# Chunks 0 and 1 of a banded-attention kernel computed as dense blocks on TensorE, with the gate weights decoded first

## The chip, the core and the metric

The kernel runs on one core of a Trainium2 chip. The metric is device time in microseconds of one execution of the whole program. A core has five engines that run their own instruction queues in order and wait for each other by semaphores: TensorE (PE; its weight loads are listed as PEld), VectorE (DVE), ScalarE (ACT), GpSimd (POOL) and SyncE (SP, which here only issues DMAs). Matmul results go to PSUM, which this kernel divides into three pools, `ps_a` (3 buffers), `ps_h` (3) and `ps_o` (2).

## What is computed

Inputs are q, k, v of shape (8 batches, 8 heads, 576 positions, 64) and the weights of a gated feed-forward network, all float32 at the reference; the kernel's weights arrive as float64 bit patterns and are decoded on chip.

```
def _attn_ref(q, k, v):
    q_d, k_d, v_d = means of q, k, v over groups of 4 positions       # 144 positions
    out_up = repeat(softmax(q_d k_d^T / 8) v_d, 4)                    # "coarse" part
    mask = |i - j| < 4
    out_local = softmax(where(mask, q k^T / 8, -1e9)) v               # "banded" part
    return out_up + out_local

x = attn rows, one row of 8 heads * 64 = 512 numbers per token, 4608 tokens
xn = x / sqrt(mean(x*x) + 1e-6) * rms_g
out = (silu(xn @ w_gate) * (xn @ w_val)) @ w_out                       # 512 -> 1536 -> 512
```

## The kernel before

The 4608 tokens are cut into 18 chunks of 256. A chunk is not 256 neighbours: a "unit" takes positions 4u to 4u+3 of each of 16 segments of 36 positions, for two batches, and chunk c holds units 2c and 2c+1 (`j` = 0, 1). Each chunk has three parts.

**Coarse part** (`Coarse`, one object per batch and head pair, 32 in all, 8 of them for batches 0 and 1, which chunks 0 to 4 need): `scores` (PE, L499), `peak` and `scale` (DVE, L508, L513), `powers` (ACT, L518), `turn` (PE transposes, L527), `copy` (ACT, L534), `values` (PE, L541), `invert`, `scaled` (DVE) and `store` (a DMA from ACT's queue to a DRAM tile `up`). Its inputs are sums of q and k, and of v, over 4 positions. For batches 0 and 1 `OpeningSums` loads the four addends (`raw_qk`, 1.18 MB each, `raw_v`) into places that the decoded weights take later (`wo`, `wv`, `wg`), adds q and k by identity products on PE (`add`, L408) with a copy on ACT (L420), and v on POOL and DVE (L429). For later batches POOL's accumulating DMAs add them.

**Banded part** (`Attention`): per chunk 8 products of 128x896 on DVE (`score`, L757) with a sum each (`score_sum`, L761), a softmax on small tiles, then the weighted values as 7 terms per output, made by ACT (`value_scalar`, L804), DVE and POOL (`value`, L811), and added by DVE (`value_sum`, L830), for chunks 0 and 1 by identity products on PE (L826). `load_up` (ACT's queue, L839) reads the coarse results back from DRAM, `add_up` (DVE, L845) adds them, then come `squares` (ACT, L855), `mean` (PE, L862), `rms` and three Newton steps `root` (DVE or POOL), `norm` (DVE, L894), `turn` (PE, L906), `high` (ACT, L910) and `low` (DVE, L914), which leave the transposed chunk as a rounded part `xh` and its rest `xl`.

**Feed-forward part** (`Forward`): for each of 12 blocks f of 128 hidden columns: `first(f, 0)` (the gate product, 12 matmuls of 256 columns, L975), `tanh` (ACT, L982), `first(f, 1)` (the value product, 12 matmuls), `gate` and `product` (DVE, L985, L990), `high` (ACT, L996), `low` (DVE or POOL, L999), and `second(f)` two blocks later (6 matmuls of 512 columns, L1010). At the end two copies on ACT (L1017) and two stores of the output (L1020).

**Weights.** 36 pieces of 0.52 MB (24 of `w_gate` and `w_val`, 12 of `w_out`) are loaded by SP and decoded (`load_weight`): `scale` on ACT (L254), `last_bits` on POOL (L264), `join` on DVE (L271), `high` on ACT (L283, L281), `split` on DVE or POOL (L295, L293, L291). Block f = 0 of chunk 0 needs the 8 pieces of its group; every third piece of the first 24 is one of `w_out`. A rounded weight may be written once the users of its place (`used`) are done.

**Order.** A planner (`Plan`) decides the order of chunks 0 to 2: each piece of work is a task with an engine, a cost, a due time and its inputs and buffers; the planner walks through time and starts the earliest possible task, the one with the smallest due time among equals. The engines then run the queues that result. `due` holds the chunks' due times, `MB` the planner's time for a megabyte of DMA. From chunk 3 on the order is written out by hand and arranged by the compiler's own scheduler.

## Time and profile before

| | us |
|---|---|
| median of 3 runs (1148.75, 1149.18, 1151.49) | 1149.18 |
| the profiled execution | 1145.97 |
| its span, from first to last instruction | 1144.2 |
| first gate matmul of chunk 0 starts at | 108.89 |
| store of chunk 0's output issued at | 188.17 |
| store of chunk 1's, 2's, 3's, 4's output issued at | 256.08, 318.72, 375.88, 446.80 |

In the profile a line such as `L975 PE MATMUL ps_h<-xh,wg 128*128 128x256 f32 x1728 | 348.2, 283 | ...` is a group of instructions: source line, engine, operation, tile written and tiles read, shape, count, then busy time in us and the mean duration of one in ns, then how long the engine was idle just before them and who ended that. A stage table gives for each stretch of time the busy time of every engine, the TensorE clock that was granted (1.00 is full) and the share of the DMA engines in use. The chain of waits is followed back from the last instruction. Durations of instructions on one engine overlap a little, so that the groups of a stretch add up to more than its busy time.

### The profile page before, as it was taken

What the parts mean: (1) busy time and instruction counts of PE and PEld (TensorE: products, weight loads), DVE (VectorE), ACT (ScalarE), POOL (GpSimd) and SP (SyncE); (2) the same over time, 40 slices, a digit from 0 to 9 for tenths busy, and PEclk for the clock granted to TensorE, in tenths of its full rate; (3) what the DMA queues carried; (4) which work ended last, traced back from release to release, by engine and by line L of the source; (5) the groups of instructions that cost most, each with busy time, mean ns of one, the idle gap of its engine ahead of it and who ended that gap; (6) DMA issues with size and microseconds to landing.
All of it is one profiled execution on the core that took longest, in us unless ns stands there. A gap on an engine that the chain in (4) does not pass through costs nothing.

```text
span 1144.2 us, 22238 instructions
## 1 busy us (share of the span) xinstructions
PE 1082.0 (95%) x8002; PEld 990.2 (87%) x8002; DVE 927.7 (81%) x1869; ACT 624.1 (55%) x2284; POOL 255.7 (22%) x317
## 2 busy tenths in 40 slices
PE   6883799999999899999999999999999999999998
PEld 4772698888899899999999999999999999999997
DVE  6787898778889989797979797979798989887432
ACT  1574673747392847474747474747475573837221
POOL 1554562334221211111111111101011020201000
PEclk9885999999999999999999999999999999999999
DMA  9985482446535353535263535222231313220000
GB/s 264 301 275 170 102 227 76 95 101 149 127 87 117 99 115 88 115 87 115 83 120 87 115 88 114 78 64 75 66 91 46 105 52 99 68 58 20 1 19 19
DMA packets 76815, 119.59 MB, mean 105 GB/s; under 512 B 26784, under 2 KB 36256, under 8 KB 76704
## 3 DMA queue, kind: packets, MB, share of 16 engines
q1 hardware_dynamic: 47520, 97.34, 28.8%
q0 software_dynamic: 8640, 15.93, 9.0%
q10 hardware_dynamic: 20544, 4.89, 2.0%
q8 instruction: 63, 1.03, 0.4%
q14 instruction: 48, 0.39, 0.1%
HBM read 106.33 MB, written 11.80 MB: 103 GB/s over the span
## 4 chain that ended last, share of the span: by engine, by line
PE 76%; DVE 9%; DMA 8%; ACT 3%; issue 3%; SPq 1%; POOL 1%; ACTq 0%; DVEq 0%; POOLq 0%
PE ps_h L975 46%; PE ps_o L1010 23%; PE ps_a L541 2%; DMA wg<-in_v_sum_dram 2%; DMA qk<-in_qk_sum_dram 2%; PE ps_a L499 2%; ACT prod L804 1%; DMA vs<-in_v_sum_dram 1%; PE ps_a L906 1%; DVE prod L757 1%; DVE o_sb L271 1%; PE ps_a L527 1%; DMA kv<-in_k_pad_dram 1%; DVE sc L761 1%; DMA up<-o_g 1%
## 5 line engine op out<-in xcount | busy, mean ns | idle before, releaser
L1010 PE MATMUL ps_o<-wo,hs 128*128 128x512 f32 x1296 | 356.0, 399 | 4.2 <-POOL hs L999 3.7
L975 PE MATMUL ps_h<-xh,wg 128*128 128x256 f32 x1728 | 348.2, 283 | 4.8 <-ACT xh L910 2.3
L975 PE MATMUL ps_h<-xh,wv 128*128 128x256 f32 x1728 | 343.0, 281 | 4.6 <-DVE sil L985 4.5
L975 PEld LDWEIGHTS ps_h<-xh,wg 128*128 128x128 f32 x1728 | 282.9, 190 | 14.2 <-ACT xh L910 3.0
L975 PEld LDWEIGHTS ps_h<-xh,wv 128*128 128x128 f32 x1728 | 281.9, 189 | 10.8 <-DVE sil L985 6.9
L804 ACT ACTIVATE prod<-kv,sc 128x64 f32<-128x64 f32 x1072 | 281.7, 408 | 13.0 <-DVE sc L795 4.8
L1010 PEld LDWEIGHTS ps_o<-wo,hs 128*128 128x128 f32 x1296 | 221.9, 188 | 41.4 <-POOL hs L999 6.2
L975 PE MATMUL ps_h<-xl,wg 128*128 128x256 f32 x864 | 244.8, 283 | 0.1
L975 PE MATMUL ps_h<-xl,wv 128*128 128x256 f32 x864 | 241.5, 280 | 0.0
L982 ACT ACTIVATE sil<-ps_h 128x256 f32<-128x256 f32 x216 | 82.9, 384 | 233.9 <-PE ps_h L975 208.8
L811 POOL TENSOR_TENSOR prod<-sc,kv 128x256 f32<-128x256 f32 x144 | 116.4, 843 | 397.4 <-DVE sc L795 175.4
L985 DVE SCALAR_TENSOR_TENSOR sil<-sil,ps_h 128x256 f32<-128x256 f32 x216 | 89.7, 415 | 103.1 <-ACT sil L982 91.0
L975 PEld LDWEIGHTS ps_h<-xl,wg 128*128 128x128 f32 x864 | 164.1, 190 | 6.9 <-issue 1.3
L975 PEld LDWEIGHTS ps_h<-xl,wv 128*128 128x128 f32 x864 | 163.6, 189 | 1.8
L996 ACT ACTIVATE hs<-sil 128x256 fp32r<-128x256 f32 x216 | 89.5, 416 | 136.9 <-DVE sil L990 122.4
L757 DVE TENSOR_TENSOR prod<-q_t,kv 128x896 f32<-128x896 f32 x140 | 151.7, 1086 | 5.6 <-DMA q_t<-in_q_band_dram 5.2
L830 DVE TENSOR_REDUCE x_t<-prod 128x128 f32<-128x896 f32 x128 | 136.8, 1077 | 23.6 <-ACT prod L804 16.4
L761 DVE TENSOR_REDUCE sc<-prod 128x14 f32<-128x896 f32 x144 | 154.5, 1077 | 0.4
L999 DVE TENSOR_TENSOR hs<-sil,hs 128x256 fp32r<-128x256 f32 x196 | 91.4, 466 | 29.5 <-ACT hs L996 29.2
L990 DVE SCALAR_TENSOR_TENSOR sil<-sil,ps_h 128x256 f32<-128x256 f32 x216 | 89.9, 416 | 8.1 <-PE ps_h L975 6.4
L362 POOL DMA_DIRECT2D qk<-in_qk_sum_dram x36 | 32.2, 895 | 187.3 <-DMA qk<-in_qk_sum_dram 111.8
L811 DVE TENSOR_TENSOR prod<-sc,kv 128x128 f32<-128x128 f32 (+2 forms) x144 | 69.5, 515 | 1.6 <-PE ps_o L826 0.8
(118 smaller groups left out, 984.3 us busy)
## 6 DMA issues: line engine op xcount, KB each, us to landing
kv<-in_k_pad_dram SPq DMA_DIRECT2D x72, 320.0 KB
kv<-in_v_pad_dram SPq DMA_DIRECT2D x72, 320.0 KB
qk<-in_qk_sum_dram POOLq DMA_DIRECT2D x36, 288.0 KB, 5.3
out_dram<-o_sb SPq DMA_DIRECT2D x36, 256.0 KB
q_t<-in_q_band_dram SPq DMA_DIRECT2D x70, 128.0 KB
vs<-in_v_sum_dram POOLq DMA_DIRECT2D x36, 144.0 KB, 3.5
qk<-in_qk_sum_dram SPq DMA_DIRECT2D x12, 288.0 KB
wo<-in_qk_sum_dram SPq DMA_DIRECT2D x2, 1152.0 KB
```

Of the source, the lines that this page charges most:

```text
L757: nc.vector.tensor_tensor(out=pr, in0=bcast(q[:, s0:s0 + 2], 2, NO), in1=window(k, s0), op=ALU.mult)
L761: nc.vector.tensor_reduce(out=self.sc[:, j, par, s0:s0 + 2], in_=self.pr[i], axis=AX.X, op=ALU.add,)
L804: nc.scalar.activation(out=self.pr[i][:, o, s], in_=self.v[j, par][:, s0 + s + o], func=AF.Copy, scale=p[:, s, o:o + 1],)
L811: (nc.vector if engine == "DVE" else nc.gpsimd).tensor_tensor(out=self.pr[i][:, a:b], in0=bcast(p[:, :, a:b].rearrange("p s o -> p o s"), ...
L830: nc.vector.tensor_reduce(out=self.x[j][:, s0:s0 + 2, par], in_=pr.rearrange("p o s d -> p s d o"), axis=AX.X, op=ALU.add,)
L975: nc.tensor.matmul(out=self.p[f][:, t], lhsT=wi(f)[:, 0, k], rhs=xi[:, k], start=(n == 0), stop=(n == 3 * KT - 1),)
L982: nc.scalar.activation(out=self.sil[f], in_=self.p[f][:, 0], func=AF.Tanh, scale=0.5)
L985: nc.vector.scalar_tensor_tensor(out=self.sil[f], in0=self.sil[f], scalar=1.0, in1=self.p[f][:, 0], op0=ALU.add, op1=ALU.mult,)
L990: nc.vector.scalar_tensor_tensor(out=self.sil[f], in0=self.sil[f], scalar=0.5, in1=self.p[f][:, 1], op0=ALU.mult, op1=ALU.mult,)
L996: nc.scalar.activation(out=self.hs[f][:, 0], in_=self.sil[f], func=AF.Copy)
L999: (nc.gpsimd if engine == "POOL" else nc.vector).tensor_tensor(out=self.hs[f][:, 1], in0=self.sil[f], in1=self.hs[f][:, 0], op=ALU.subtract,)
L1010: nc.tensor.matmul(out=self.o[j], lhsT=lhs[:, cols], rhs=rhs(f)[:, 0], start=(f == 0 and i == 0), stop=(f == NF - 1 and i == 2),)
```

## The change

- **Banded part of chunks 0 and 1** (new class `Dense`). For one batch b, a chunk has 128 tokens (16 segments of 8 positions). For each batch and head pair: `gather` (ACT) picks the 128 queries of the chunk out of `raw_qk`; `scores` (PE) makes, for each of the two heads, a 128x256 block of all queries against the 16 keys around each of the 16 segments: a product that writes the mask (0 or -1e30), a small one that masks the left edge of the sequence (chunk 0 only), and the product of q with k, read with strides from `raw_qk`; `peak` (DVE, two reductions and a scale), `powers` (ACT, two exponentials with their sums), `turn_a` (PE, four transposes), `copy` (ACT, 128x512) and `values` (PE, four products with v). v is loaded by 66 small DMAs of up to 16 rows x 8 heads x 64 numbers (`load_v`). The masks and a 0/1 spread matrix are made on POOL.
- **Coarse part for batches 0 and 1.** Results stay on chip (in a free part of `wo`'s place); `spread_up` adds up each chunk's rows by a product with the spread matrix. They are still stored to `up` for chunks 2 to 4, now by SP. The sums of q and k are made by three DVE additions of 128x576 instead of products on PE and copies on ACT.
- **Normalisation of chunks 0 and 1.** A token is one row, so its mean square comes from ACT's sum, without the `mean` product; `turn` multiplies with strided columns of the identity, which also puts the tokens of two batches in the order that later stages expect.
- **Weights.** The order of pieces is four of `w_gate` for f = 0 to 3, four for f = 4 to 7, four of `w_val` for f = 0 to 3, then four of `w_out`, and so on. The gate product of a block waits for gate pieces alone, the value product for value pieces. `scale` now waits, as `high` did, for the users of the weight's place; `used["wv"]` and `used["wo"]` hold all dense scores and value products of both chunks.
- **Planner:** due times 62, 118, 173 instead of 70, 125, 180, `MB` 3.6 instead of 3.1, some costs.

Not in the core below: the planner's numbers, `peak`, `powers`, `invert`, `scaled`, `squares`, `norm`.

```diff
+    class Dense:
+        def plan(self, warm_bufs, warmed):
...
+            for b in range(2):
+                for hp in range(KT):
+                    n = 4 * b + hp
+                    tag = ("ps_a", "ps_h")[n % 2]
+                    ps, pt, A, AT = [buf(tag) for _ in range(2)], buf(tag), buf("dense_a"), buf("dense_t")
+                    gather = task("ACT", 0.25, lambda b=b, hp=hp: self.gather(b, hp), at - 10, [sums_.got])
+                    scores = task(
+                        "PE", 1.15, lambda b=b, hp=hp, tag=tag: self.scores(b, hp, tag), at, [gather, rounded, stores, warmed, *self.order[-1:]],
+                        allocs=[*ps, A, AT], uses=[mask, self.bufs[3], *warm_bufs, sa, sl, *self.more],
+                    )
+                    used["wo"].append(scores)
+                    used["wv"].append(scores)
...
+        def masks(self):
+            nc.gpsimd.memset(m, 0.0)
+            for pattern, base, sign in (... four half-planes ...):
+                nc.gpsimd.affine_select(
+                    out=m, in_=m, pattern=pattern, compare_op=ALU.is_ge, fill=NEVER, base=base, channel_multiplier=sign,
+                )
...
+        def scores(self, b, hp, tag):
+            for par, ps in enumerate(self.s[b, hp]):
+                nc.tensor.matmul(out=ps, lhsT=warm["some"][:, :P], rhs=d.mask_r, start=True, stop=False)
...
+                k = bass.AP(tensor=tensor, offset=at - 1, ap=[part, [UPP, NSEG], [1, 4], [step, FAC]])
+                rows = slice(par * D, (par + 1) * D)
+                nc.tensor.matmul(
+                    out=ps, lhsT=self.q[b, hp][rows], rhs=k[rows],
+                    start=False, stop=True,
+                )
...
+        def spread_up(self, b):
+            up = self.up[b] = ps_a.tile([P, DM], FP32, name="ps_a")
+            for hp in range(KT):
+                og = self.coarse[4 * b + hp].og
+                for c in range(2):
+                    at = D * (1 - c)
+                    nc.tensor.matmul(
+                        out=up[:, hp * P:(hp + 1) * P], lhsT=(self.prev or self).made[self.c][:HALF, at:at + P], rhs=og[:, :, c],
+                        start=(c == 0), stop=(c == 1),
+                    )
...
-            for t in range(2):
-                p = buf(tag)
-                add = task("PE", 2.3, lambda t=t: self.add(t), at, got[:1], allocs=[p])
+            for j in range(1, FAC):
+                add = task(
+                    "DVE", 0.68, lambda j=j: self.add(j), at, [got[0], add],
+                    allocs=[self.qk_buf] if j == 1 else [], uses=[self.qk_buf],
+                )
...
-            nc.scalar.dma_start(
+            (nc.sync if self.b < 2 else nc.scalar).dma_start(
                 out=up_dram[self.b // 2][self.b % 2, self.hp].rearrange("t (c p) d -> p t c d", c=2), in_=self.og,
             )
...
+    order = [(0, i) for i in (*range(4), *range(8, 12), *range(4, 8))] + [(1, f) for f in range(4)]
+    order += [(0, i) for i in range(12, 16)] + [(1, f) for f in range(4, 8)]
+    order += [(0, i) for i in range(16, 24)] + [(1, f) for f in range(8, 12)]
...
-        own = joined[:24] if n >= 24 else used["wo"] if n not in gained else used["wg"] + used["wv"]
+        own = joined[:24] if n >= 24 else used["wo"] if n not in gained else used["wv" if gained[n] % 8 // 4 else "wg"]
...
+        scaled = task("ACT", 0.67, scale, at, [got, *own], allocs=[w], uses=[raw])
```

**How the queues change, at three places.** First SP's queue (DMA issues) around the last loads of the opening's sums (`in_qk_sum`, `in_v_sum`). Before, the value rows of chunk 0's band (`kv`) follow, then the first weight pieces (`in_w_...`):

```order
L396 DMA wv_0_203<-in_qk_sum_dram 128x4x576
L402 DMA wg_0_192<-in_v_sum_dram 72x4x512
L568 DMA kv<-in_v_pad_dram 128x1x640 x4
L250 DMA wg_1_295<-in_w_gate_dram 128x1024
L250 DMA wg_1_295<-in_w_val_dram 128x1024
L250 DMA wg_1_337<-in_w_out_dram 128x1024
```

Now, with the coarse stores (`up<-wo`) on the same queue and the small value loads (16x8x64):

```order
L564 DMA up<-wo_0_115 72x4x64
L408 DMA wg_0_340<-in_v_sum_dram 72x4x512
L402 DMA wv_0_183<-in_qk_sum_dram 128x4x576
L408 DMA wg_0_340<-in_v_sum_dram 72x4x512
L564 DMA up<-wo_0_115 72x4x64
L1078 DMA kv<-in_v_pad_dram 16x8x64 x16
L564 DMA up<-wo_0_115 72x4x64
L1078 DMA wv_0_166<-in_v_pad_dram 16x8x64 x8
L1078 DMA wv_0_183<-in_v_pad_dram 16x8x64 x8
L254 DMA wg_1_548<-in_w_gate_dram 128x1024
```

The first weight piece now stands behind the small loads and three of the coarse stores, which wait for DVE.

Second, PE's queue at the start of chunk 0's feed-forward part. Before: the end of the coarse part (`ps_h<-hs`), the mean product, chunk 0's transposes, the gate product:

```order
L541 MATMUL ps_h<-hs,a_g 72x64 x8
L862 MATMUL ps_a<-ss,same_sb 128x8
L906 MATMUL ps_a<-ident_sb,x_t 128x128 x8
L975 MATMUL ps_h<-xh,wg_0_408 128x256
L975 MATMUL ps_h<-xl,wg_0_408 128x256
```

Now, where `ps_o<-...,prod` are the last dense value products of chunk 1, L1204 the transposes of chunk 0, L1168 the spread products of chunk 1:

```order
L1145 MATMUL ps_o<-wv_0_166,prod 128x64
L1145 MATMUL ps_o<-wv_0_183,prod 128x64
L1204 MATMUL ps_a<-ident_sb,x_t 128x64 x16
L1168 MATMUL ps_a<-wo_0_115,sil 128x128 x8
L1168 MATMUL ps_a<-wo_0_130,sil 128x128 x8
L1269 MATMUL ps_h<-xh,wg_0_660 128x256
```

The whole dense part of both chunks now stands ahead of the first gate product.

Third, ACT's queue at the same place, now: the last copies and exponentials of chunk 1 (L1137, L1123), then the first pieces of `w_val` (L258, and L287 into `wv`) around chunk 0's `high` (L917):

```order
L1137 COPY prod<-ps_a 128x512
L1123 ACTIVATE xh,z_b<-ps_h,m_b 128x256 x2
L1137 COPY prod<-ps_h 128x512
L258 ACTIVATE o_sb<-wg_1_548 128x512 x2
L917 CAST xh<-ps_a 128x4x128
L287 ACTIVATE wv_0_1190<-o_sb,g_sb 128x4x128
L917 CAST xh<-ps_a 128x4x128
```

Before, pieces of both `w_gate` and `w_val` had been written ahead of this place in turn; now the pieces of `w_val` start here, behind the last dense exponential.

More of the change, by code (lines that the diff above doesn't have):

```diff
@@ L48 @@
 NEAR = 0.15
-MB = 3.1
+MB = 3.6
 LAND = 2.0
@@ L1053, in decode @@
         )
-        scaled = task("ACT", 0.67, scale, at, [got], allocs=[w], uses=[raw])
         bits = task(
```

324 lines of the change are left out of this document (270 added, 54 removed).

## The prediction

> **What bounds the kernel now.** I read the page first, then a table of five stages, then the chain of waits of the opening, then groups of instructions per engine.
>
> From the page:
>
> ```profile
> span 1144.2 us, 22238 instructions
> PE 1082.0 (95%) x8002; PEld 990.2 (87%) x8002; DVE 927.7 (81%) x1869; ACT 624.1 (55%) x2284; POOL 255.7 (22%) x317
> DVE  6787898778889989797979797979798989887432
> PEclk9885999999999999999999999999999999999999
> ```
>
> PE is busy for nearly the whole span, but the first four of the forty slices are DVE's as much as PE's, and there the granted clock falls to 0.5. So the program has an opening and a long PE-bound rest. The stage table, cut at the first gate matmul of chunk 0, at the store of chunk 0's output and at that of chunk 4's:
>
> ```profile
> core 0: us, PE busy (x) PEld busy (x) DVE busy (x) ACT busy (x) POOL busy (x), PEclk, DMA share, GB/s
> 0.00:40.00 40.00, 27.09 (x138) 21.11 (x138) 26.38 (x36) 8.53 (x28) 8.56 (x10) 1.00 0.96 264
> 40.00:80.00 40.00, 33.47 (x279) 29.30 (x281) 36.33 (x59) 26.78 (x87) 27.85 (x30) 0.85 0.97 322
> 80.00:108.90 28.90, 9.16 (x59) 7.29 (x56) 20.06 (x42) 14.01 (x42) 13.36 (x12) 0.50 0.55 173
> 108.90:188.20 79.30, 70.52 (x484) 63.94 (x485) 68.16 (x116) 47.38 (x118) 39.35 (x40) 0.95 0.54 137
> 188.20:446.80 258.60, 248.62 (x1893) 225.29 (x1892) 223.25 (x441) 157.80 (x621) 73.57 (x108) 0.99 0.46 106
> 446.80:1144.20 697.40, 693.14 (x5158) 643.26 (x5156) 553.47 (x1180) 369.62 (x1391) 93.05 (x118) 1.00 0.30 76
> ```
>
> In the last stage PE idles 4 of 697.4 us; nothing that the change touches runs there, so it is a constant. The stage before it has 10 us of idle PE in 258.6. Chunk 0's own feed-forward stage takes 79.3 us, against 57 us between later stores; DVE, with the weight decoding, is busy for 68.2 of them. The opening, 108.9 us, has DVE busy 82.8, ACT only 49.3. Its chain of waits and marks:
>
> ```profile
> 18.32 20.97 DMA wg<-in_v_sum_dram
> 88.16 4.50 DMA up<-o_g
> 93.68 3.88 DMA up_t<-up
> 109.62 2.50 PE ps_h L975 x10
> ...
> 108.89 0.58 PE L975 MATMUL ps_h<-xh,wg 128*128 128x256 f32 x1 [0.68 <-ACT xh L910]
> ```
>
> Inputs arrive until 39 us; near the end the coarse results go to DRAM and come back (88 to 97.6 us) and the rest is a chain of small steps.
>
> **The change, part by part.** I price it by four stages: to the first gate matmul; to chunk 0's store; to chunk 4's; to the end. Prices come from these groups of DVE and of ACT, both of 0 to 188.2 us:
>
> ```profile
> L761 DVE TENSOR_REDUCE sc<-prod 128x14 f32<-128x896 f32 x20 | 21.6, 1079 | 0.3
> L757 DVE TENSOR_TENSOR prod<-q_t,kv 128x896 f32<-128x896 f32 x16 | 17.8, 1110 | 5.4 <-DMA q_t<-in_q_band_dram 5.2 <-issue 0.2
> L811 DVE TENSOR_TENSOR prod<-sc,kv 128x512 f32<-128x512 f32 (+1 forms) x16 | 12.6, 790 | 0.8 <-PE ps_o L826 0.8
> L295 DVE SCALAR_TENSOR_TENSOR wg<-o_sb,g_sb,wg 128x512 fp32r<-128x512 f32 x12 | 11.5, 961 | 0.7 <-ACT wg L283 0.7
> L271 DVE SCALAR_TENSOR_TENSOR o_sb<-o_sb,wv 128x512 uint32<-128x512 uint32 x12 | 9.6, 826 | 0.0
> L508 DVE TENSOR_REDUCE m_g<-ps_h 72x2 f32<-72x288 f32 x8 | 3.3, 438 | 0.6 <-PE ps_h L499 0.6
> L513 DVE TENSOR_SCALAR m_g<-m_g 72x4 f32<-72x4 f32 x8 | 3.6, 454 | 0.2
> L845 DVE TENSOR_TENSOR x_t<-ps_o,up_t 128x512 f32<-128x512 f32 x2 | 1.3, 686 | 5.4 <-DMA up_t<-up 5.4
> ...
> L804 ACT ACTIVATE prod<-kv,sc 128x64 f32<-128x64 f32 x48 | 13.1, 337 | 5.0 <-PE ps_o L826 1.9 <-PE ps_a L826 1.9 <-DVE sc L795 1.0
> L283 ACT ACTIVATE wg<-o_sb,g_sb 128x512 fp32r<-128x512 f32 x12 | 8.6, 717 | 1.6 <-DVE o_sb L271 1.6
> L254 ACT ACTIVATE o_sb<-wg 128x512 f32<-128x512 f32 x12 | 7.7, 665 | 1.2 <-DMA wg<-in_w_gate_dram 0.6 <-DVE wg L295 0.5
> L518 ACT ACTIVATE a_g<-ps_h,m_g 72x144 f32<-72x144 f32 x16 | 5.8, 371 | 3.9 <-DVE m_g L513 2.9 <-PE ps_h L527 1.1
> L982 ACT ACTIVATE sil<-ps_h 128x256 f32<-128x256 f32 x12 | 4.6, 380 | 7.7 <-PE ps_h L975 7.4
> L518 ACT ACTIVATION_READ_ACCUMULATOR a_g<-ps_h,m_g 72x1 f32 x16 | 3.1, 196 | 0.0
> L910 ACT CAST xh<-ps_a 128x512 fp32r<-128x512 f32 x4 | 2.3, 584 | 7.9 <-PE ps_a L906 7.9
> ```
>
> *Removed.* DVE loses 16 products and 16 sums of two chunks (16 x 1.11 + 16 x 1.08 = 35.0 us), 16 value products (12.6) and two softmaxes on small tiles (some five steps each of L513's kind, 0.45: 4.5): 52 us. ACT loses 48 scalings (13.1). PE loses the identity products; the mean product and the trip through DRAM leave the chain of chunk 0.
>
> *Added on DVE.* 12 additions of 128x576 at 0.686 x 576/512 = 0.77: 9.2 us. 16 dense peaks, each two reductions of 128x256 (nearest L508, 0.44) and a small scale (L513, 0.45): 21.3. Four `scaled` at 0.69 and four inversions at 0.6: 5. Over the program's start DVE is relieved by 52 - 36 = 16 us.
>
> *Added on ACT.* 32 dense exponentials, each a 128x256 read of PSUM (L982, 0.38) and a read of the sum (0.196): 18.4. 16 copies of 128x512 (L910, 0.585): 9.4. 16 gathers, unknown, between L804's 0.34 for half the columns and the copy's 0.585; I take 0.35: 5.6. ACT gains 33 us and loses the 13 us of scalings and a few of copies and squares; all of the additions fall before the first gate matmul, 32 of the 48 scalings fell after it.
>
> *Stage 1.* I count DVE's queue up to chunk 0's last `low` with these prices: additions 9.2; 48 reductions 21.1; 36 small scales and 12 reciprocals 17.8; 8 coarse results and 8 additions of v 8.8; 8 of 512 columns 5.5; 10 joins 8.2; 8 splits 7.5; Newton steps and norms 4.2; one score 1.1: 83 us. The old stage's groups add up to 89.7 us by the same reckoning where the table has 82.8 busy, a factor 0.92, so 77 us busy. ACT's queue to the same place: 32 coarse exponentials of 0.57 18.1, dense ones 18.4, copies 9.4 and 6.3, gathers 5.6, 10 scales 6.7, 9 gate or value weights 6.5, the rest 6.5: 77.5 us, where it was 49.3. So two engines now have the same load. DVE can start when the first sum has landed, some 7.5 us (the first q and k, 0.45 MB, ended DVE's first idle time, 5.2 us in L757's row, and this load has 1.18 MB). Bounds: below, no later waits, 7.5 + 77.5 = 85; above, DVE idle as long as before (26 us) and 7 us more because ACT has no slack, 77 + 26 + 7 = 110. The idle 26 had 9 for the DRAM trip and its tail, which goes; two full engines that hand each other 24 items will not run without gaps. I take 99: gain 10 us.
>
> *DMA and SP in that stage.* 6.3 MB of band inputs go, 2.1 MB in pieces of 256 bytes come. The queues in 0 to 80 us, and one SP issue:
>
> ```profile
> q1 hardware_dynamic: 9089, 22.85, 92.9%
> q10 hardware_dynamic: 2076, 0.53, 3.1%
> ...
> 29.11 0.59 SPq L250 DMA_DIRECT2D wg<-in_w_gate_dram  x1
> ```
>
> A packet of q1 (2.5 KB) takes 0.929 x 16 x 80 / 9089 = 131 ns, one of q10 (255 bytes) 19 ns: 19.2 against 13.4 GB/s per engine. So 6.3 MB less is 20.5 us, 8192 small packets more 9.8 us. SP issues 66 small loads at 0.35 to 0.6 us, 23 to 40 us, so the first weight piece goes out near 41 us instead of 29. Its join stands behind some 36 us of other work in DVE's queue, due near 45 us, so this costs at most 4 us, inside the bounds. The Trainium skill (DMA: Bandwidth & Descriptors, "Specifications") gives 512 bytes as the least transfer for line rate. The trace agrees in kind, 13.4 against 19.2 GB/s. If that rule meant half rate, an estimate from that page, the small loads would take 14 us instead of 9.8, and the weights would come 4 us later.
>
> *Stage 2.* Before, 79.3 us with DVE idle 11. The value weights now start behind the last dense scores: from the first gate matmul to the first `product` stand 14.0 us of DVE work, then 57.9 to the last of chunk 0 (26 joins and 16 splits of weights, 13 band instructions of chunk 2). 71.9 x 0.92 = 66 busy, plus the same idle, 77. Gate-first brings forward only 12 matmuls. Bounds 71 (idle 5) and 84 (idle 18). Gain 2.
>
> *Stage 3.* Chunk 2's band is 14 of 16 instructions along at chunk 0's store, it was 8 (L761's 20 sums less 16 of chunks 0 and 1, twice): 6.5 us less for DVE while PE has 10 us of idle to regain. I take 3; bounds 10 of gain, since no more is idle, and 4 of loss, the planner's new order being otherwise unpriced. 255.6.
>
> *Sum:* 99 + 77 + 255.6 + 697.4 = 1129.0 of span. The profiled execution was 1145.97, 1.8 more than its span, and the median 3.2 above that: **1134 us**. Least 85 + 71 + 248.6 + 697.4 + 5 = 1107; most 110 + 84 + 262.6 + 697.4 + 5 = 1159.
>
> **The rivals.** *Packed opening.* ACT and DVE run almost without gaps, first gate at 89, chunk 0 in 71, stage 3 gains 8: 1113. For it: the four quarters of the input arrive by 35 to 39 us and there is always another head pair to work on. Against: in 40 to 80 us DVE, with data at hand, was busy 36.3 of 40, so gaps of a tenth are usual.
>
> *The debt of the decoding.* At the first gate matmul 10 pieces are joined, where it was 14. If the opening gains 5 us (104) and chunk 0 then waits for value weights with 18 us of idle DVE (84), chunk 0 is stored at 188, as before, and the end is 1148 to 1149: no change. For it: the value pieces' whole decoding now starts after the last dense exponential. Against: DVE has less to do in both stages.
>
> *Dense items in single file.* An item holds a set of PSUM buffers (`ps_a` or `ps_h`) from its scores to its copy, and goes PE, DVE, ACT, PE, ACT, PE. For a coarse item the chain shows:
>
> ```profile
> 50.74 0.69 PE ps_a L499 x8
> 53.70 1.04 ACT a_g L518 x6
> ```
>
> 4.0 us from scores to the end of the exponentials, and the turn, copy and values follow. With 24 items and two sets, if a set takes 9.4 us per item, the opening ends at 7.5 + 24 x 4.7 = 120, and the sum is 120 + 77 + 258.6 + 697.4 + 5 = 1158: slower. It decides from 4.2 us per item on ((108.9 - 7.5)/24). Against it: ACT and DVE work is 3.2 us per item, and the next scores need only the exponentials' buffers.
>
> **How the numbers follow.** The forecast has 0.55, with an own range of 1124 to 1145; the packed opening 0.13; the debt 0.15; single file 0.17. A measurement of this kernel tells changes of about 0.3%, here below 1145.7 or above 1152.6. Faster: the first two and a third of the debt's, with a little of the forecast's upper end against it, 0.73. Same 0.11, slower 0.16. For 8 in 10 the range reaches from the packed case to near the single file's: 1113 to 1155.
>
> **What would show it.** The first gate matmul between 94 and 105 us, with ACT busy for over 70 of them; the first `product` 10 to 13 us behind it; chunk 0's store at 171 to 182; chunk 4's at 428 to 438; 697 us from there. Clock 0.5 should no longer stand for 29 us before the first gate matmul, since PE has the dense part there. I am wrong if the first gate matmul comes after 108, or if chunk 0 then takes over 85 us, or if chunks 1 to 3 give the gain back.

## The result, and the profile after

The changed kernel takes 1206.85 us (median of 4 executions) against 1148.97 before: slower, ratio 1.050 with a 95% interval of 1.045 to 1.055. The forecast was 1134, its range 1113 to 1155. Of all executions reported below one, the profiled one of e17, took 3778 us, with its products two to three times as long (677 ns for 283 at 256 columns) at a granted clock recorded as 1.00; nothing explains it. The page of the profiled execution (1206.48 us), as before: busy times, then tenths of forty slices of 30 us:

```profile
span 1204.7 us, 22541 instructions
PE 1165.8 (97%) x8142; PEld 1053.1 (87%) x8142; DVE 905.3 (75%) x1888; ACT 633.3 (53%) x2299; POOL 234.9 (19%) x305
PE   7999989798999999999999999999999999999998
DVE  4444358867688999798898979797979889897432
PEclk8555559898999999999999999999999999999999
```

The first five slices have turned round: PE is nearly full there, DVE below half, and the granted clock is 0.5 for five slices, where before it was below 0.9 in three, of these at 0.5 in one. The stage table, cut at the same events (40 and 80 us, first gate matmul, stores of chunks 0 and 4):

```profile
core 0: us, PE busy (x) PEld busy (x) DVE busy (x) ACT busy (x) POOL busy (x), PEclk, DMA share, GB/s
0.00:40.00 40.00, 31.66 (x187) 24.78 (x188) 17.36 (x39) 17.09 (x59) 6.39 (x16) 0.80 0.63 168
40.00:80.00 40.00, 38.09 (x182) 30.42 (x181) 19.11 (x47) 17.80 (x64) 8.70 (x11) 0.50 0.67 208
80.00:166.30 86.30, 84.95 (x339) 66.32 (x338) 32.42 (x83) 32.71 (x88) 14.63 (x20) 0.52 0.45 123
166.30:246.70 80.40, 67.91 (x428) 60.02 (x428) 67.48 (x113) 42.59 (x89) 38.12 (x36) 0.87 0.42 119
246.70:506.50 259.80, 249.17 (x1852) 227.26 (x1851) 211.82 (x425) 151.96 (x599) 73.56 (x104) 0.97 0.45 104
506.50:1204.70 698.20, 694.04 (x5166) 644.36 (x5164) 557.07 (x1182) 371.15 (x1403) 93.48 (x118) 1.00 0.30 76
```

The span is 60.5 us longer. 57.4 of them stand ahead of the first gate matmul (166.3 instead of 108.9; the record of that matmul itself starts at 165.95); the other stages are within 1.2 us of before (80.4, 259.8, 698.2 against 79.3, 258.6, 697.4). In the opening PE is busy for 154.7 of 166.3 us, DVE for 68.9, ACT for 67.6. What PE waited for from 20 us to there (total, times, longest, in us):

```profile
PE ps_a L530 <- ACT a_g L521: 2.4, 2, 2.2
PE ps_h L530 <- ACT a_g L521: 1.5, 1, 1.5
PE ps_o L1145 <- ACT prod L1137: 1.4, 2, 0.7
```

Parts of the chain of waits there (start, us, what):

```profile
35.28 6.53 DMA wg<-in_v_sum_dram
41.84 0.70 DVE hs L428
...
47.97 1.17 PE ps_h L1110 x2
...
128.10 0.85 PE ps_h L1132 x4
128.95 0.21 PE ps_h L1102
129.16 1.17 PE ps_h L1110 x2
130.33 0.51 PE ps_h L1102
130.84 1.17 PE ps_h L1110 x2
132.01 1.90 PE ps_o L1145 x8
...
152.54 6.83 PE ps_a L1204 x32
159.36 6.93 PE ps_a L1168 x32
```

Until 42 us the chain waits for the last addends of the sums, whose load stands on SP's queue behind small loads of v; from 48 us on it is nearly all PE. A dense item is mask, key product, mask, key product (128.95 to 132.01, 3.06 us), eight value passes (1.90) and four turns (0.85): 5.8 us of PE at clock 0.5, 16 times. A full-precision product is two passes: the x2 in 1.17 us is one key product of one head.

### The profile page after: what moved, and what is told of

The parts are those of the page before. It is cut to its first block, busy times and chain, and to the rows that moved or that the text cites. A ratio compares the mean times of both kernels' runs of the same rounds, so it can differ in the third digit from the quotient of the medians.

```text
span 1204.7 us, 22541 instructions
## 1 busy us (share of the span) xinstructions
PE 1165.8 (97%) x8142; PEld 1053.1 (87%) x8142; DVE 905.3 (75%) x1888; ACT 633.3 (53%) x2299; POOL 234.9 (19%) x305
## 4 chain that ended last, share of the span: by engine, by line
PE 86%; DMA 5%; DVE 4%; ACT 2%; issue 1%; POOL 1%; SPq 1%; ACTq 0%; DVEq 0%; POOLq 0%
PE ps_h L1269 47%; PE ps_o L1304 23%; PE ps_a L544 2%; PE ps_o L1145 2%; PE ps_a L502 2%; PE ps_h L1110 1%; DMA wv<-in_qk_sum_dram 1%; PE ps_a L1168 1%; PE ps_a L913 1%; PE ps_a L1110 1%; PE ps_a L530 1%; PE ps_a L1204 1%; SPq L1078 1%; ACT a_g L521 1%; DVE o_sb L275 1%
## 5 line engine op out<-in xcount | busy, mean ns | idle before, releaser
L1269 PE MATMUL ps_h<-xh,wv 128*128 128x256 f32 x1728 | 348.3, 282 | 7.3 <-DVE sil L1279 3.5
L1269 PE MATMUL ps_h<-xh,wg 128*128 128x256 f32 x1728 | 352.3, 284 | 0.5 <-DVE wg L299 0.5
L1269 PEld LDWEIGHTS ps_h<-xh,wv 128*128 128x128 f32 x1728 | 284.7, 191 | 13.9 <-DVE sil L1279 4.9
L811 ACT ACTIVATE prod<-kv,sc 128x64 f32<-128x64 f32 x1024 | 269.5, 411 | 12.4 <-DVE sc L802 4.9
L818 POOL TENSOR_TENSOR prod<-sc,kv 128x256 f32<-128x256 f32 x128 | 104.2, 842 | 407.8 <-DVE sc L802 204.9
L1290 ACT ACTIVATE hs<-sil 128x256 fp32r<-128x256 f32 x216 | 89.1, 415 | 124.6 <-DVE sil L1284 109.1
L764 DVE TENSOR_TENSOR prod<-q_t,kv 128x896 f32<-128x896 f32 x128 | 139.9, 1095 | 0.9 <-PE ps_o L1145 0.7
L768 DVE TENSOR_REDUCE sc<-prod 128x14 f32<-128x896 f32 x128 | 136.9, 1075 | 0.1
L1293 DVE TENSOR_TENSOR hs<-sil,hs 128x256 fp32r<-128x256 f32 x198 | 87.3, 442 | 26.7 <-ACT hs L1290 26.2
L818 DVE TENSOR_TENSOR prod<-sc,kv 128x128 f32<-128x128 f32 x128 | 56.3, 476 | 0.9
```

The source lines that it names most:

```text
L764: nc.vector.tensor_tensor(out=pr, in0=bcast(q[:, s0:s0 + 2], 2, NO), in1=window(k, s0), op=ALU.mult)
L768: nc.vector.tensor_reduce(out=self.sc[:, j, par, s0:s0 + 2], in_=self.pr[i], axis=AX.X, op=ALU.add,)
L811: nc.scalar.activation(out=self.pr[i][:, o, s], in_=self.v[j, par][:, s0 + s + o], func=AF.Copy, scale=p[:, s, o:o + 1],)
L818: (nc.vector if engine == "DVE" else nc.gpsimd).tensor_tensor(out=self.pr[i][:, a:b], in0=bcast(p[:, :, a:b].rearrange("p s o -> p o s"), ...
L1269: nc.tensor.matmul(out=self.p[f][:, t], lhsT=wi(f)[:, 0, k], rhs=xi[:, k], start=(n == 0), stop=(n == 3 * KT - 1),)
L1290: nc.scalar.activation(out=self.hs[f][:, 0], in_=self.sil[f], func=AF.Copy)
```

## The experiments

Times are medians of at least four executions; "first gate" is the first gate matmul in the profiled execution.

### Is PE the bound of the opening? (e3, e2)

Two additions to `scores`, ahead of each mask product, in e3 (first line; the lines that name `k` and `rows` are left out) and e2 (last two):

```diff
+                nc.tensor.matmul(out=ps, lhsT=self.q[b, hp][rows], rhs=k[rows], start=True, stop=True)   # e3
+                for _ in range(4):                                                                       # e2
+                    nc.tensor.matmul(out=ps, lhsT=warm["some"][:, :P], rhs=d.mask_r, start=True, stop=True)
```

> The control to the run with added rounded products: the changed kernel with the 64-row product of q and k of every dense score made twice (the first overwritten), 32 more products of the strided kind, 0.585 us each from start to start at clock 0.5. T1, and TensorE as the bound of the opening: these bring no clock, the opening is longer by their 18.7 us, first gate matmul 185, 1225 us. Rival (the opening is bound by the hand-over between engines or by the landing of inputs, TensorE only looks busy): less than half of it shows, below 1216 us.

> The changed kernel with four more rounded 256-column products (the mask's own, overwritten by it) ahead of each dense score, 128 in all; the planner's costs and the order stay. One such product took 0.21 us from start to start at clock 0.5. T1: the added streaming brings the clock back to 1.0 in most of 20 to 160 us, the 145 us of half-clock work there shrink to about 75 plus 14 of added products, the first gate matmul comes at 100 to 125 us instead of 166 and the time is 1140 to 1165 us. T2 (waits) and T3 (amount of work): the clock stays 0.5, the opening is longer by 128 x 0.21 = 27 us, the first gate matmul at 193, 1234 us.

e3: 1225.08 us, first gate 184.95, 19.0 later than without (165.95). The size is right, though the expectation had reached it by a slip: a product is two passes of 0.585 us, so 32 are 37 us. The timeline of e3 shows why 19 are left:

```profile
151.93 0.58 PE L1109 MATMUL ps_a<-sil,hs 128*128 128x256 f32 x1
152.44 0.79 PE L1117 MATMUL ps_a<-wv 64*128 64x256 f32 x1
152.45 0.79 PE L1105 MATMUL ps_a<-wv 64*128 64x256 f32 x1
153.06 0.62 PE L1117 MATMUL ps_a<-wv 64*128 64x256 f32 x1
```

The second head's added product (L1105) stands next to the first head's own (L1117) and uses the other 64 rows: both run at once. So one added product per item costs time, 16 x 1.17 = 18.7 us, and all of it shows in the time. PE is the bound.

e2: 1224.46 us. 128 added products would cost 27 us at clock 0.5; they cost 18 by the median and 9 in the profiled execution (first gate 175.2, mean clock from 20 us to there 0.63 instead of 0.55). Neither theory as written: the filling lifts the clock in places, but not for good.

### What lowers the clock? PE alone (e1, e5, e9)

These kernels leave out everything but products on tiles that lie on the chip; no product waits for another engine. A score in them, `r` being 64 rows or all 128, `x` the keys with a stride or packed:

```python
mm(ps[par][:, :C], rr[:, :P], rr[:, :C], True, False)            # mask: rounded, 256 columns
mm(ps[par][:, :FAC], ident_sb, kc[:, :FAC], False, False)        # edge: 4 columns
mm(ps[par][:, :C], q[r, n % 8], x, False, True)                  # key product
```

> This kernel computes nothing of the reference: TensorE alone runs stages of 32 to 128 products of one kind from tiles that lie on the chip, with no wait on another engine, each stage behind 36 or more rounded 256-column products (stages: 256 rounded columns; 288 columns with the identity; 256 full-precision columns with 128 rows, with 64 rows, and with 64 rows read with the dense scores' stride; 64 columns with new weights; the 128x128 turn; 72 rows and 128 columns; the coarse kinds; then whole dense items as the changed kernel has them, with 2, 4 and 8 more rounded products ahead of each score, and with the keys packed). Theory T1 (the granted clock follows how much the array streams; small, 64-row or strided full-precision products with new weights each do not hold it): clock 1.0 in the stages of 256 and 288 columns with 128 rows, 0.5 for most of the stages with 64 rows and stride, 64 columns and the plain dense item, and 1.0 again at some number of added rounded products. Rival T2 (the clock fell because TensorE had short waits between items): 1.0 in every stage, since there are no waits here. Rival T3 (the clock is no cause, only the amount of TensorE's work): also 1.0 in every stage, and a dense item takes about the 5.6 us that it took in the changed kernel.

> Again TensorE alone without waits, nothing of the reference computed. Each stage behind 36 or more rounded products. Stages in order: the dense scores alone as in the changed kernel (mask, edge, then a 64-row product that reads the keys with a stride, for each head); without the edge product; with the two heads' key products next to each other; with packed keys; the turns and value products alone; the coarse items alone; then dense and coarse items together with strided keys, with packed keys, and with packed keys and the two heads next to each other. The first run with TensorE alone showed that every single kind holds clock 1.0, that the whole dense item with strided keys falls to 0.5 after 12 us and that with packed keys it does not. Theory T1b (what lowers the clock is the lone 64-row product on strided keys: half of the rows, and a column every second clock, so that the array is mostly idle while TensorE counts as busy): 0.5 in the first two stages and in the mix with strided keys, 1.0 in all others. Rival T5 (the change between kinds of product lowers it, whatever the stride): 0.5 also in the last two stages, 1.0 in those of the scores alone only where they are of few kinds.

> TensorE alone, nothing of the reference computed. The clock is granted in steps of 3.41 us. Counting each pass of a product as its columns (twice for full precision) times its share of the 128 rows, the ten runs so far have 583 steps in the openings and in the stages of TensorE alone: of 320 steps below 2800 counted clocks none was followed by clock 1.0, of 214 above 3300 all but one were, whatever the clock in the step itself. Theory T1c: the gate goes by this count, with its edge near 3050 in 3.41 us, 0.37 of what the array can do at the full clock, 0.75 of what it can do at half. Stages here: packed dense scores alone with 64 rows (at the full clock 784 counted in 1.06 us, 2520 a step), the same with all 128 rows in the key product (same durations, 1296 in 1.06 us, 4170 a step), then the 64-row ones with 1, 2, 3 and 4 more rounded products per item (2795, 3050, 3270, 3460 a step), strided keys with 64 rows (1785) and with 128 rows (2950), then 288 products of 64 columns (3940) and 360 of 72 rows and 64 columns (3780). T1c: 0.5 in the 64-row stage, 1.0 with 128 rows, 0.5 with 1 more, either with 2, 1.0 with 3 and 4, 0.5 with stride and 64 rows, either with stride and 128, 1.0 for the whole of the last two. Rival T5 (mixed kinds): the 128-row stage falls as the 64-row one does, since kinds and order are the same. Rival T6 (a delay only: every weak kind falls if it lasts long enough): the last two fall after 25 us.

Four of the fifteen stages of e1 (columns as in the stage table): 192 value passes; six dense items as in the kernel (their turns made as two-pass products); the same with four more rounded products a score; the same with packed keys.

```profile
100.00:121.30 21.30, 21.30 (x194) 21.30 (x193) 0.00 (x0) 0.00 (x0) 0.00 (x0) 1.00 0.01 2
202.20:239.50 37.30, 37.30 (x156) 28.46 (x155) 0.00 (x0) 0.00 (x0) 0.00 (x0) 0.66 0.00 0
296.70:330.20 33.50, 33.50 (x198) 24.06 (x198) 0.00 (x0) 0.00 (x0) 0.00 (x0) 1.00 0.00 1
379.40:402.40 23.00, 23.00 (x154) 18.82 (x153) 0.00 (x0) 0.80 (x3) 0.00 (x0) 1.00 0.00 1
```

All ten stages of a single kind hold 1.0, strided 64-row products included, so T1 in its first form is wrong. But whole dense items fall to 0.5 with PE never idle (with two more rounded products a score too: 0.57), so waits (T2) are not needed, and the clock is not incidental (T3). Then e5: dense scores alone with strided keys; with packed keys; dense items (packed) and coarse items in turn.

```profile
18.30:84.60 66.30, 66.30 (x180) 41.23 (x178) 0.00 (x0) 0.00 (x0) 0.00 (x0) 0.54 0.00 0
211.10:282.40 71.30, 71.30 (x198) 45.85 (x198) 0.00 (x0) 0.00 (x0) 0.00 (x0) 0.53 0.00 0
433.70:473.90 40.20, 40.20 (x394) 34.46 (x394) 0.00 (x0) 0.00 (x0) 0.00 (x0) 1.00 0.01 1
```

T1b blamed the stride and was wrong too: packed scores fall as well (18 strided items take 66.3 us, 20 packed ones 71.3, at clock 0.5 the same 1.8 us a head). The same scores with strided keys of two neighbouring heads also fell (clock 0.54 in that stage); turns and values alone and coarse items alone held 1.0, and with strided keys the mix of dense and coarse items had 0.62. Then e9, in this order: packed scores with 64 rows; the same with all 128 rows in the key product; strided with 64 rows; strided with 128.

```profile
18.20:73.50 55.30, 55.30 (x158) 35.55 (x157) 0.00 (x0) 0.00 (x0) 0.00 (x0) 0.55 0.00 1
83.10:107.40 24.30, 24.30 (x161) 22.68 (x159) 0.00 (x0) 0.00 (x0) 0.00 (x0) 1.00 0.00 1
377.40:421.10 43.70, 43.70 (x120) 26.95 (x118) 0.00 (x0) 0.00 (x0) 0.00 (x0) 0.55 0.00 0
430.90:459.40 28.50, 28.50 (x121) 17.71 (x119) 0.00 (x0) 0.00 (x0) 0.00 (x0) 1.00 0.00 1
```

The rows of the key product decide. The same sixteen items take 24.3 us with 128 rows and 55.3 with 64, and the clock holds in the one and falls in the other. T5 (mixed kinds) is out with that, and T6 (a delay) with the last two stages of e9, which held 1.0 for 64 and 47 us. T1c was wrong on one stage: with three more rounded products an item the clock fell (0.57) where it said 1.0; with one and two it fell, with four it held.

The expectation took the durations to be equal; they are not. Even at clock 1.0 a packed head takes 1.06 us from mask to mask with 64 rows (first items of that stage) and 0.76 with 128 (24.3 / 32). The Trainium skill (TensorEngine Tiling (Array Packing), "Key Properties") says that changing the tiling mode drains TensorE; these durations agree with it.

The clock itself: it changes only in steps of 3.41 us. For each step of the openings of all the kernels here but e17, and of the three runs with PE alone, the passes that start in it are counted: columns, twice for full precision, times the share of the 128 rows (a full-precision product has two passes). The fullest step holds 4352 at clock 0.5 and 8320 at 1.0. Of 595 steps below 2800 all but one were followed by clock 0.5, of 398 above 3300 all but one by 1.0, whatever the clock in the step itself; of the 84 between, 31 were followed by 1.0 and 53 by 0.5.

Counting the share of the rows is needed: with the edge at 3050, 25 of the 1077 steps stand on the wrong side, and without that share the best edge leaves 124. The busy share does not tell the two apart: of the 804 steps in which PE was busy for 99% or more, 351 were followed by 1.0 and 453 by 0.5. The edge is thus at 0.7 of the fullest step at clock 0.5, and the changed kernel's opening mostly does 1000 to 2900 there while PE is called busy. This is a count fitted to the runs (the stage of e9 that T1c missed fell behind a step of 3120, inside the band); what the hardware counts isn't shown. The Trainium skill (TensorE: Matmul & The Clock Gate, "What's actually happening") says that one busy window of about 3.4 us releases the clock. The window agrees, "busy" does not: PE was busy for 84.95 of 86.3 us at 0.52.

### Mending the key product (e6, e7, e8, e16, e18)

e6 has a packed copy of the keys, made by ACT; e7 also puts the two heads' key products next to each other; e8 is e7 with the copies on POOL; e16 is e6 with q written once per head, zeros in the other head's rows, so that the product runs over 128 rows; e18 has these zeros and no packed keys. (Lines of the products are joined here.)

```diff
+            copy(                                                                  # e6, e7, e8, e16
+                out=k.rearrange("p (s e t) -> p s e t", e=4, t=FAC),
+                in_=bass.AP(tensor=tensor, offset=at - 1, ap=[part, [UPP, NSEG], [1, 4], [step, FAC]]),
+            )
-                nc.tensor.matmul(out=ps, lhsT=self.q[b, hp][rows], rhs=k[rows], start=False, stop=True)
+                nc.tensor.matmul(out=ps, lhsT=self.q[b, hp][:, par], rhs=k, start=False, stop=True)  # e16, e18
```

> The changed kernel with one thing else: ScalarE copies the keys of a dense item into a packed 128x256 tile (four such tiles in turn, 16 copies of some 0.4 us), and the dense score reads that. T1b: the clock goes back to about 1.0 in most of 20 to 160 us; a dense item takes 3.8 us of TensorE instead of 6.2 (both from the run with TensorE alone), 16 of them save 38 us, and the coarse items and spreads run at the full clock as well; the first gate matmul comes at 105 to 125 us instead of 166, and the time is 1145 to 1165 us. Rival T5 (mixed kinds keep the clock low): the clock stays near 0.5 and the time within 10 us of 1207.

> As the run with packed keys, and the key products of the two heads of an item stand next to each other, so that the two halves of the rows can run at once (0.108 us a pass in place of 0.216 in the run with TensorE alone). T1b: a further 0.43 us for each of 16 items, 7 us, where TensorE is still the bound: first gate matmul at 98 to 118, 1138 to 1158 us. If TensorE is no longer the bound by then, VectorE and ScalarE with 69 and 68 us of work plus the copies are, and the two packed runs differ by under 3 us. T5: as the changed kernel less 16 x 0.9 us, about 1190 us.

> As the run with packed keys and neighbouring heads, but the copies on GpSimd (a 128x256 step there took 0.84 us) in place of ScalarE. T1b: if ScalarE's 6 to 7 us of copies stand on the path, this is up to 6 us faster than on ScalarE; if not, the same within 4 us; if GpSimd's 14 us hold up the first items, up to 6 us slower.

> The changed kernel with packed keys (as in the run that took 1209 us) and q written twice, once per head, with the other head's 64 rows as zeros (written once by GpSimd), so that each key product runs over all 128 rows; the sums are the same. With TensorE alone a packed score with 128 rows took 0.76 us a head and held clock 1.0, with 64 rows 1.06 and fell to 0.5; the stage of 64 rows, at half clock, took 1.73 us a head (55.3 us for 32). Theory T1c with T9 (a product on half of the rows between products on all rows drains the array, which costs time and count): an item takes 0.6 us less at the full clock and 1 us or more less at half, and counts 4600 instead of 3600; first gate matmul 125 to 148 instead of 162, mean clock from 20 us to it above 0.62 (0.55 with 64 rows), 1170 to 1195 us. Rival T10 (the packed run was slow for another reason than the half rows): within 6 us of 1209.

> The changed kernel with the zero rows alone: q padded as in the run before it in this list, keys read with the stride as in the changed kernel, no key copies. With TensorE alone a strided score took 1.19 us a head with 128 rows and held clock 1.0, 1.50 with 64 rows and 0.5 (1.82 there). T9: 16 items save 1.0 us each or more, first gate matmul 138 to 155 instead of 166, 1182 to 1200 us. T10: within 6 us of 1207.

| | us | first gate | mean clock, 20 us to it | from there to chunk 0's store | on to chunk 4's |
|---|---|---|---|---|---|
| changed kernel | 1206.85 | 166.0 | 0.55 | 80.4 | 259.8 |
| e6 packed | 1208.73 | 162.1 | 0.55 | 74.5 | 271.9 |
| e7 packed, neighbours | 1186.17 | 130.6 | 0.71 | 76.4 | 267.6 |
| e8 the same, copies on POOL | 1191.93 | 148.8 | 0.59 | 73.8 | 270.7 |
| e18 128 rows, strided | 1187.52 | 142.5 | 0.70 | 77.6 | 273.0 |
| e16 128 rows, packed | 1181.64 | 136.8 | 0.65 | 76.7 | 271.2 |

(e7's profiled execution took 1173.64, its shortest, 12.5 less than its median; its other columns are of that one.) Packing alone does next to nothing, as with PE alone at clock 0.5. The change of rows, with the same sums, gives 19 us on strided and 27 on packed keys: e16 lies within what T9 expected in time, first gate and clock, e18 in time and first gate, and T10 is out. (PE's queue up to the first gate matmul is in the same order in e6 and e16 but for one product; in e18 its later half is ordered otherwise than in the changed kernel, so part of the 19 may be the order's.) Neighbouring heads gain 23 us on the packed keys. T1b's times for e6 and e7 were not reached; T5's were (within 10 us of 1207, about 1190), although e5 and e9 rule its mechanism out. Copies on POOL cost 6 us. The stages of e16 (to the first gate matmul, to chunk 0's store, to chunk 4's):

```profile
0.00:136.80 136.80, 117.53 (x703) 100.66 (x703) 67.70 (x169) 81.70 (x240) 29.58 (x51) 0.70 0.64 182
136.80:213.50 76.70, 62.66 (x387) 54.49 (x387) 64.31 (x103) 41.30 (x80) 38.15 (x39) 0.87 0.51 134
213.50:484.70 271.20, 258.92 (x1901) 235.48 (x1900) 215.75 (x440) 157.60 (x623) 73.15 (x104) 0.96 0.44 100
```

The opening is 29.5 us shorter, chunk 0's stage 3.7, and then the next stage is 11.4 longer (271.2 against 259.8). The queues have moved work: PE has 41 passes fewer in chunk 0's stage (387 for 428) and 49 more in the next (1901 for 1852). The shorter opening is not what does it, since e6 has the same with an opening of 162; against e6 the opening is 25.3 us shorter and the two stages together only 1.5 longer, so nearly all of it is paid out.

### Filling steps (e10, e11, e17)

e7 with two more rounded products a score (e10); with twelve on the third and fourth item (e11); e16 with twelve there and none elsewhere (e17).

```diff
+                for _ in range(12 if self.slot[b, hp] in (2, 3) else 2):
+                    nc.tensor.matmul(out=ps, lhsT=warm["some"][:, :P], rhs=d.mask_r, start=True, stop=True)
```

> As the run with packed keys and neighbouring heads (first gate matmul at 131, 1186 us), with two more rounded products ahead of each dense score, 64 in all. T1c: at clock 0.5 an item then counts some 4600 in 6.0 us, 2620 a step, still below the edge, so the clock comes back only where spreads or turns help; once up it stays (4600 in about 3.9 us). The mean clock from 20 us to the first gate matmul 0.65 to 0.85, the first gate matmul at 120 to 138, 1175 to 1195 us. Rival (TensorE's work is what counts, the clock is no lever): 64 x 0.21 = 14 us more, 1200 us.

> As the run with two more rounded products, but twelve in place of two ahead of each score of the third and fourth dense item (at some 28 and 45 us), so that each of these items has a step that is filled: 24 x 256 = 6144 counted clocks. T1c: the clock goes up to 1.0 at one of them and holds for most of what follows, mean clock from 20 us to the first gate matmul 0.8 or more, first gate matmul at 105 to 122, 1155 to 1178 us. Rival (amount of work): 40 products more than the run with two, 4 to 9 us slower than that.

> As the run with 128-row products, with twelve more rounded products ahead of each score of the third and fourth dense item (48 in all) and none elsewhere. T1c: two steps filled, each followed by a stretch of 1.0; mean clock 0.1 higher than without, first gate matmul 3 to 12 us earlier than without them, 1163 to 1188 us. Rival (amount of work): 48 x 0.21 = 10 us later.

e10: 1180.88 us, first gate 138.8, mean clock 0.66; e11: 1178.52, 134.9, 0.76. e11's clock, first gate and time all miss what was expected (0.8, 105 to 122, 1155 to 1178), the time by half a microsecond. The clock does go up at both filled steps of e11 (34 and 51 us), as T1c says, but falls again after 10 and 7 us; in these stretches PE is busy for 8.4 of 10.3 and 6.0 of 6.8 us. From 20 us to the first gate matmul PE waits 13.9 us in all for ACT, DVE and POOL. Added work is paid back, hardly more: 1179 to 1181 against 1186. e17: 1184.84 us, 3 over e16, inside T1c's range and 7 short of its rival's; without a first gate matmul to compare, it decides nothing.

### The other parts of the change (e4, e12, e13, e14, e15)

e4 and e12 are the kernel before with the sums on VectorE alone, and with gate weights decoded first alone (the lines of the change's diff). e13 is the changed kernel with the old order of the weights, e14 is e11 with it, and e15 is that with five bursts (3rd, 4th, 6th, 8th and 10th item) and no other filling.

```diff
-    order = [(0, i) for i in (*range(4), *range(8, 12), *range(4, 8))] + [(1, f) for f in range(4)]
+    pieces, place = [], {}                                                                # e13, e14, e15: as before
...
-        scaled = task("ACT", 0.67, scale, at, [got, *own], allocs=[w], uses=[raw])
+        scaled = task("ACT", 0.67, scale, at, [got], allocs=[w], uses=[raw])
```

> The kernel before with one part of the change alone: the sums of q and k of the first two chunks on VectorE instead of 32 identity products of 288 columns on TensorE and their copies on ScalarE. T1: TensorE loses the heavy stream that held the clock at 1.0 between 20 and 41 us, so the clock is 0.5 there; but it has little else to do in that opening, so the time changes little: VectorE gets 9 us of additions, first gate matmul 109 to 118, 1149 to 1158 us. Rival T4 (the loss of these identity products alone explains the result): first gate matmul beyond 140, above 1180 us.

> The kernel before with another part of the change alone: the gate weights of a column group are decoded ahead of the value weights, the value product of the first chunk waits for its own four pieces, the output weights' pieces come behind, and a piece is scaled only when its place is free; the planner's numbers and everything else as before. The prediction put 2 us of gain on this in the stage of chunk 0's feed-forward part and nothing in the opening. T1c says nothing of it. If the reordering itself delays the opening, the first gate matmul comes later than 112 us; expected: 106 to 111, time 1140 to 1152 us.

> The changed kernel with one part undone: the weights are decoded in the order of the kernel before (gate and value pieces in turn, output pieces between). Before alone with the new order took 1161 us, 15 more than before: first gate matmul at 113 instead of 109, chunk 0's stage 83 instead of 79, the next 267 instead of 259. Theory T7 (the new order costs as much here): the first gate matmul 162 to 168 as in the changed kernel, TensorE being the bound until then, and 4 to 10 us less in the two stages behind it: 1194 to 1205 us. Rival T8 (with an opening of 166 us DVE has caught up with the decoding, so that the order is worth nothing): within 3 us of 1207.

> The run with packed keys, neighbouring heads, two more rounded products a score and two bursts (first gate matmul at 135, 1178.5 us; chunk 0's stage 71.5 us, the next 272.9 instead of 258.6), with the old order of decoding. T7: the same first gate matmul within 4 us, and the stage to chunk 4's store 5 to 14 us shorter: 1163 to 1175 us. T8-like rival (the 272.9 us come from the shorter opening itself: VectorE owes the same decoding, whatever its order): no more than 3 us from 1178.

> As the run before it in this list, but twelve more rounded products ahead of each score of the 3rd, 4th, 6th, 8th and 10th dense item and none ahead of the others: 120 in place of 104. T1c: each burst is a step that is filled, so the clock returns to 1.0 after every fall: mean clock from 20 us to the first gate matmul 0.85 or more (0.76 with two bursts), the first gate matmul at 118 to 130, and 3 to 10 us less than with two bursts. Rival (the gaps in TensorE's work, not its clock, now set the opening): the clock is higher but the first gate matmul stays within 4 us of 135.

e4: 1156.61 us, ratio 1.0068 (1.0039 to 1.0097); the clock falls to 0.5 from 12 to 60 us without the identity products, the first gate matmul comes at 110.4. T4 is out: these products alone explain 9 of the 58 us, and in the profiled execution (1161.75) hardly any of it in the opening; chunk 0's stage is 89.1 us there instead of 79.3. e12: 1161.29, ratio 1.0116 (1.0066 to 1.0165), where I expected 1140 to 1152. Its stages:

```profile
0.00:113.10 113.10, 70.79 (x472) 57.30 (x472) 81.21 (x137) 48.44 (x154) 40.89 (x48) 0.82 0.86 247
113.10:196.30 83.20, 74.14 (x482) 66.77 (x482) 73.10 (x114) 48.33 (x120) 42.55 (x43) 0.92 0.55 140
196.30:462.90 266.60, 252.51 (x1882) 228.37 (x1882) 216.71 (x443) 152.75 (x604) 72.81 (x103) 0.98 0.44 101
```

That is 4, 4 and 8 us more than before.

e13: 1209.39, no difference from the changed kernel, so T8's number and not T7's. But not T8's account either: in the profiled execution (1212.78) the first gate matmul comes at 176.5, 10.5 later, and the stages up to chunk 4's store take 337.4 us together instead of 340.2. e14: 1187.44, 9 slower than e11: T7 has the wrong sign, its rival (within 3 us of 1178) misses too, and the claim behind it (that the order costs 15 in any surroundings) falls. With the old order the first gate matmul comes later (158.5 in place of 134.9) and the stages up to chunk 4's store are shorter (329.2 us together against 344.4). Why the new order costs 15 us in the kernel before and nothing here stays open.

e15: 1183.88, 3.6 less than e14 as T1c had it, but with a mean clock of 0.74 and not 0.85, and a first gate matmul at 154.4, which in the old order compares with e14's 158.5. Bursts lift the clock for 7 to 31 us, then it falls. PE waits 21.9 us for other engines from 20 us on; that these gaps by then set the time too is its rival's point, which is argued and not shown.

No version beats the kernel before; of those with the dense blocks e16 (2.6% slower, interval 2.2 to 3.0) and e11 (2.8%, 2.6 to 3.0) come nearest.

## Why the prediction was wrong, point by point

- **The step that failed: the opening's price.** Stage 1 was priced on DVE, ACT and the transfers: two queues of 77 us, 99 with their gaps. The engines' prices were fair (DVE 68.9 and ACT 67.6 us busy; a dense peak's reduction 0.424 us for 0.44 taken, an exponential 0.47 for 0.38, a copy 0.584 for 0.585, a gather 0.43 for 0.35, an addition 0.76 for 0.77; only the dense scale was far off, 0.17 for 0.45). SP's queue was not: the first weight piece went out at 62.1 us and not near 41, as 16 of the small loads alone held the queue for 16.0 us. PE had no term, and so even the upper sum, 1159, lies 48 below the result. The profile of before could have given a bound: it has 70 us of PE in the opening (27.09, 33.47 and 9.16), and every dense item adds 18 to 22 passes.
- **How large the missing term is.** At clock 1.0, from the runs with PE alone: strided scores 32 x 1.50 = 48.0, value passes 128 x 0.111 = 14.2, turns 64 x 0.111 = 7.1, eight coarse items 8 x 2.02 = 16.2, the spread 64 x 0.111 = 7.1, chunk 0's turn 3.6, the rounded idle products 3.9: about 100 us (2 less, since chunk 1 has no edge product), more than either queue that was priced, and 105 to 107 behind a start at 7. So even at the full clock this opening had next to nothing to gain on 108.9. This sum is an estimate of mine; no run shows this opening at clock 1.0. Measured, at clock 0.5 from 31 us on but for one step, it was 154.7.
- **The clock.** "Clock 0.5 should no longer stand for 29 us before the first gate matmul, since PE has the dense part there" was the wrong way round: the dense part is what kept it at 0.5, 0.50 and 0.52 from 40 to 166 us. The prediction took a busy PE for one that gets its clock.
- **The strided keys** were never priced either: a strided pass took half a microsecond even at clock 1.0 (timeline of the scores alone in e5, first items):

```profile
18.36 1.13 PE L97 MATMUL ps<-raw,q 64*128 64x256 f32 x2
19.43 0.39 PE L97 MATMUL ps<-rr 128*128 128x256 f32 x1
19.65 0.28 PE L97 MATMUL ps<-kc,ident_sb 128*128 128x4 f32 x2
19.86 1.14 PE L97 MATMUL ps<-raw,q 64*128 64x256 f32 x2
```

  The two passes of a key product and their drain take 1.07 us from start to the next mask, of 1.50 us for a head; packed, two such passes took 0.63.
- **Stages 2 and 3.** Predicted 77 and 255.6; measured 80.4 and 259.8, no gain. Gate-first is not worth 2 us: alone it cost 15. In e6, e7, e11 and e16 chunk 0's stage does shrink, to 71.5 to 76.7, and the next grows to 268 to 273, 344 to 348 together against 338 before. This is not the debt of the decoding, the second rival, as it was written: at the first gate matmul 10 pieces are joined, as it says, but in every one of these runs all 36 are joined before chunk 0's store, and e6 shows the same growth behind an opening of 162. Work that moved between the two stages is part of it; why the two together are 6 to 10 us longer stays open. If that held behind an opening of 99 us, the end would be 99 + 344 + 697 + 5 = 1145 by an estimate from these runs, no gain that can be told.
- **The rivals.** The packed opening is far off. "Dense items in single file" had the side and the place, an opening set by 24 items in a row, but another mechanism: PE's waits from 20 us on, 5.3 us in all, are for operands and not for PSUM, and PE itself was the file, at 5.8 us for a dense item and not 4.7.
- **What held.** The last stage (698.2 for 697.4); nearly, the first `product` 13.4 us behind the gate matmul (10 to 13 given) and ACT's load (67.6 us, over 70 given).

## What to carry to other kernels

When work moves to an engine that is already busy in that stage, that engine needs a term in the sum, at both of its clocks, before the engines that are relieved get theirs. A busy TensorE is not a TensorE at full clock: products on 64 rows between products on 128 rows, read with a stride, kept it at 0.5 here for over 100 us, and zero rows, which add arithmetic, made the kernel 19 to 27 us faster. A shorter stage can come with a longer one behind it, as the planner moves work (271.2 us for 259.8 in e16); price the sum of both.

## What the runs showed of the hardware that was not expected

- A 64-row product between 128-row products costs 0.3 us more a head than one over all 128 rows (1.06 against 0.76 us at clock 1.0, e9), and two 64-row products on different halves run at the same time (started 0.01 us apart in e3).
- A full-precision pass of 256 columns that are read one by one with a stride took 0.49 us with 128 rows and 0.51 with 64 at clock 1.0, from its start to that of the second pass; packed, 0.30 and 0.32. The Trainium skill (SBUF — State Buffer, the note on cachelines under "Door 1: The DMA port swizzle") says that each access that crosses to a new 16-byte line pays a penalty; here the stride takes every column to a new line, and the durations agree.
- The granted clock followed a count of streamed columns per 3.41 us, with its edge near 3050 (0.37 of the fullest step at the full clock), in 991 of 993 steps outside a band of 8% around it.
